# Turning the mixed input by blocks: 32 small DMAs within SBUF, or six by way of a scratch in DRAM

## The chip, the core and the metric

The kernel runs on one core of a Trainium2 chip. The metric is device time in microseconds (us) of one execution. Five engines matter here: PE multiplies matrices, DVE and ACT work elementwise, POOL does a little at the start, and SP issues DMAs, which 16 DMA engines carry out. Each engine works through its own list of instructions in order, and semaphores tie the lists together.

## What is computed

A short dynamic convolution along the sequence, and after it a gated feed-forward layer:

```python
w = np.exp(weight_gen - max); w = w / (sum + 1e-09)      # batch 4, seq 4096, 8 heads, 7 taps
x_unf = x_pad[:, idx, :]                                  # 7 shifted views of x, d_model 192
attn = np.einsum('bshk,bskhg->bshg', w, x_unf)            # 16384 x 192
g = attn @ w_gate                                         # 192 -> 1536
silu = g * (1.0 / (1.0 + np.exp(-g)))
out = (silu * (attn @ w_val)) @ w_out                     # 1536 -> 192
```

## The kernel before

The 16384 tokens are worked through in 32 groups (`NG`) of 512 (`NC`), and each group in 12 steps (`NF`), one for each 128 of the 1536 hidden columns. A step is named here by its f, from 0 to 11. In each step PE makes the 128 gate and 128 value columns for the group's 512 tokens (`up_first` and `up_second`), ACT applies Silu (`sg`, L493), DVE multiplies (`h`, L507), ACT rounds the product to its high part (`hi`, L508), DVE takes the low part (`lo`, L510), and PE, two steps later (`LAG`), multiplies high and low parts by `w_out` (`down`, L537 and L546). Inputs and weights are split into high and low parts as well, so that a product is made of three.

For the next group the convolution runs beside these steps. DVE multiplies and adds seven shifted views of x (`first`, `product`, `add`; L230 and L258), 13 operations that the table `todo` spreads over the steps from f = 9 of one group to f = 5 of the next. The sum has tokens on its partitions, but PE needs the 192 channels there. The turn has these parts:

- `blocks` (L317), at f = 6: DVE transposes 32x32 blocks into the tile `cut`.
- `places` (L330), right behind: SP issues 32 DMAs of 16 KB within SBUF that carry the blocks to their places in the tile `t32` (the profile calls it `t`). Its half 0 holds channels 0 to 127, its half 1 channels 128 to 191 twice, on the upper and the lower 64 partitions.
- `split_ops` (L351, L358): `high(0)` on ACT, `low(0)` on DVE, `high(1)`, `low(1)`. They make `xhi` and `xlo` of both halves. `turn_ops` calls these four the halves.

What sets the order is the code itself: the whole list is written out under a manual schedule. In a step, PE's `up_first` comes first, then the `down` products, `up_second`, Silu and `gated`, which puts the first entry of the step's `todo` list between `hi` and `lo`; the rest of the list follows behind `lo`. With `at` = f 6, the two entries of `moves` stand at `at`, and `halves` are spread from `at + 2` to `at + 4`, that is two at f = 8 and two at f = 9. Group 1 is prepared during group 0 with shorter leads: its turn is at f = 8 and its halves at f = 10 and 11.

Of the next group, `up_first` reads half 1 first: its first two matmuls (L473) need `xhi` of half 1 and the next two `xlo` of half 1. The sums have four PSUM buffers, two for each step, so PE runs up to two steps ahead of `sg` and `h`.

SP's list also holds the loads of x (1344 KB, issued at f = 9 in every second group), of the taps, and the stores of the results (four DMAs a group, at f = 2).

Of the kernel before, what the change touches and what calls it, by code (L numbers as in the profile page):

```python
# [8 lines left out]
F32 = mybir.dt.float32  # L9
# [9 lines left out]
def dynconv_glu_kernel(  # L19
# [23 lines left out]
    nc = tc.nc  # L43
    B, S, D = x.shape
# [3 lines left out]
    P = 128  # L48
    T = B * S // P
    PAD = K - 1  # L50
    DB = D - P
    JG = 4
    NC = JG * P
# [24 lines left out]
    xts = ctx.enter_context(tc.tile_pool(name="xts", bufs=2))  # L78
    hp = ctx.enter_context(tc.tile_pool(name="hp", bufs=2))
    outp = ctx.enter_context(tc.tile_pool(name="outp", bufs=2))  # L80
    ps_up = ctx.enter_context(tc.tile_pool(name="ps_up", bufs=4, space=PSUM))
    ps_dn = ctx.enter_context(tc.tile_pool(name="ps_dn", bufs=1, space=PSUM))

# [35 lines left out]
    def load_taps(c):  # L119

        j0, n = wcuts[c]
        wt = w_t[c] = soft.tile([P, NJ, H, K], F32, tag="wt", name="wt")
        pieces = {0: (0, JG, n), 1: range(0, n + 1, 2 * JG)}.get(c, (0, n))

        def load(a, b):
            nc.sync.dma_start(
                out=wt[:, a:b].rearrange("p t h k -> p t (h k)"), in_=wgr[:, j0 + a : j0 + b]
            )

        return [lambda a=a, b=b: load(a, b) for a, b in zip(pieces, pieces[1:])]  # L130
# [174 lines left out]
    Q = 32  # L305
    NB = D // Q

    def turn_ops(g):

        whole = {}  # L310

        def blocks():
            cut = att.tile([P, JG, D], F32, tag="aside", name="cut", bufs=ASIDE)
            cut = whole["cut"] = cut.rearrange("p t d -> p (t d)").rearrange(
                "p (i t c) -> p i t c", i=NB, t=JG
            )
            nc.vector.transpose(  # L317
                cut, xatt[g][:, :, 0:D].rearrange("p t (i r) -> p i t r", i=NB)
            )

        def places():
            t32 = att.tile([P, JG, 2 * P], F32, tag="xatt", name="t32")
            t32 = whole["t32"] = t32.rearrange("p t d -> p (t d)").rearrange(
                "p (i n) -> p i n", i=2
            )
            for i in range(2 * P // Q):
                half, to = divmod(i * Q, P)
                src = i if i < NB else i - DB // Q
                for j in range(P // Q):
                    nc.sync.dma_start(  # L330
                        out=t32[to : to + Q, half, j * P : (j + 1) * P],
                        in_=whole["cut"][j * Q : (j + 1) * Q, src].rearrange("p t c -> p (t c)"),
                    )

        def part(n):
            def go():
                if n == 0:
                    t32 = whole["t32"]
                    whole["split"] = split_ops(g, (t32[:, 0], t32[:, 1]))
                whole["split"][n]()  # L340

            return go

        return [blocks, places], [part(n) for n in range(4)]

    def split_ops(g, ps):
        hi = [xts.tile([P, NC], F32R, tag=f"xhi{half}", name="xhi") for half in range(2)]

        def high(half):
            def go():  # L350
                nc.scalar.activation(out=hi[half], in_=ps[half], func=AF.Copy)  # L351

            return go

        def low(half):
            def go():
                lo = xts.tile([P, NC], F32R, tag=f"xlo{half}", name="xlo")
                nc.vector.tensor_tensor(  # L358
                    out=lo, in0=ps[half], in1=hi[half].bitcast(F32), op=ALU.subtract
                )  # L360
                xT[g, half] = hi[half], lo

            return go

        return [high(0), low(0), high(1), low(1)]
# [220 lines left out]
    def spread(ops, first, last):  # L586

        for n, op in enumerate(ops):
            at = first + (n * (last - first)) // len(ops)
            todo.setdefault(max(at, 0), []).append(op)  # L590

    with tc.manual_schedule():
        nc.gpsimd.memset(exp_bias, -920.0 * TWO23)

        nc.scalar.activation(out=warm, in_=exp_bias, func=AF.Exp)
        now, soon = load_x(0)
        for op in load_taps(0) + [now]:
            op()
        load_weights(0)
        load_weights(1)  # L600
        soon()
        for f in range(2, RAW):
            load_weights(f)
        make_identity(nc, ident)

        before, exponentials, after = softmax_ops(0)
        for op in before:
            op()
        convert = [weight_ops(f) for f in range(NF)]
        w0, w1, w2, w3 = convert[:4]  # L610
        nc.scalar.activation(out=warm, in_=exp_bias, func=AF.Silu)
        for op in after[:3]:
            op()
        ps, taps = summed_turn(attention_ops(0))
        meanwhile = w0 + w1[:2]
        for op in taps[:2]:
            op()
        for op, other in zip(meanwhile, taps[2:] + [lambda: None]):
            op()
            other()  # L620
        turns = split_ops(0, ps)
        for op in turns[0::2] + w1[2:4] + turns[1:2] + w2[:1] + turns[3:]:
            op()

        later = after[3:]
        loads = load_x(1) + load_taps(1)
        todo[0] = [w2[1], w3[0], w2[2]]
        for i in range(NF):
            ops = todo.setdefault(i, [])
            for f, part in ((i + 2, 3), (i + 3, 1), (i + 4, 0), (i + 3, 2)):  # L630
                if f < NF:
                    ops.append(convert[f][part])
        todo[0] += later[:3]
        spread(loads, LOAD1, LOAD1 + 7)
        spread(later[3:], NF - LEAD - 2, NF - LEAD)
        spread(
            [lambda f=f: split(wo[:, f, 0], wo[:, f, 1], wo32[:, f]) for f in range(NF)],
            WO,
            NF + LAG - 1,
        )  # L640
        for c in range(1, len(wcuts)):
            s0 = (wcuts[c - 1][0] // JG - 1) * NF - LEAD if c > 1 else NF
            s1 = (wcuts[c][0] // JG - 1) * NF - LEAD
            before, exponentials, after = softmax_ops(c)
            at = s0 + (s1 - s0) * 5 // 8 - 2 if c > 1 else EXP1
            if c + 1 < len(wcuts):
                todo.setdefault(s1, []).append(lambda c=c: load_taps(c + 1)[0]())
            spread(before, s0 + 1 - (c == 1), at)
            exps[at] = exponentials
            spread(after, at + 2, s1)  # L650
        for g in range(1, NG):
            s0 = (g - 1) * NF - (LEAD if g > 1 else LEAD1)
            c = first_x.get(g)
            if c and c + 1 < len(xcuts):
                todo.setdefault(s0, []).append(lambda c=c: load_x(c + 1)[0]())
            asides, rest = attention_ops(g)
            spread(asides, max(s0, 0), s0 + NF - 4)
            spread(rest, max(s0, 0), s0 + NF - 3)
            moves, halves = turn_ops(g)
            at = s0 + NF - 3  # L660
            spread(moves, at, at + 1)
            spread(halves, at + 2, at + 4)

        steps = [(g, f) for g in range(NG) for f in range(NF)]
        for i in range(len(steps) + LAG + 1):
            ops = todo.pop(i, [])
            if i < len(steps):
                g, f = steps[i]
                sums, nop = up_first(g, f)
                if i in exps:  # L670
                    exps[i]()
            if i > LAG:
                down(*steps[i - LAG - 1], 1, True)
            late = []
            if LAG <= i < len(steps) + LAG:
                s = steps[i - LAG]
                down(*s, 0, False)
                late = [(*s, 0, True)]
                if s[1]:
                    down(*s, 1, False)  # L680
                else:
                    late.append((*s, 1, False))
            if i < len(steps):
                up_second(g, f, sums, nop)
                sg = silu(sums)
            for what in late:
                down(*what)
            if i > LAG:
                h_t.pop(steps[i - LAG - 1])
            if i < len(steps):  # L690

                def between():
                    if ops:
                        ops.pop(0)()
                    return ops

                gated(g, f, sums, sg, between)
            for op in ops:
                op()
# [33 lines left out]
```

## Time and profile before

| | |
|---|---|
| time, median of 3 runs | 1760.01 us (1759.1 to 1762.0) |
| the profiled execution, its time | 1765.17 us |
| its span, first to last instruction | 1763.4 us |
| PE, DVE, ACT busy | 1420.1, 1026.6, 597.8 us |
| mean granted clock of PE | 0.89 |
| SP's 32 issues of the turn (L330), share of the chain that ended last | 33% |

The profile was taken in one execution; the time around its span is 1.8 us. A clock of 1.00 is 2.4 GHz, 0.50 is 1.2 GHz. The chain that ended last is followed back from the last instruction to whatever released each step, so an engine's share of it is time that set the end. "SPq" is SP's queue at work on issuing.

### The profile page before, as it was taken

To read this page: it belongs to the slowest core of one execution; us is meant where nothing else is said; L and a number is where in the kernel's file an instruction comes from. 1 tells how busy PE (TensorE), PEld (TensorE's weight loads), DVE (VectorE), ACT (ScalarE), POOL (GpSimd) and SP (SyncE) were. 2 spreads that over 40 slices of the span, in tenths; PEclk is the share of its full clock that TensorE was granted. 3 is DMA by queue.
4 is the path that set the end of the run, shared out by engine and by line. 5 is a ranking of instruction groups with operands and counts; after the bars stand their busy time and mean duration, and the time that the engine had idled before them with its cause. 6 is when DMAs were issued, how large, how long until landed. Compare 5 with 4: busy or idle time off the path is not lost.

```text
span 1763.4 us, 32367 instructions
## 1 busy us (share of the span) xinstructions
PE 1420.1 (81%) x13168; PEld 1311.0 (74%) x13168; DVE 1026.6 (58%) x1414; ACT 597.8 (34%) x1048; POOL 61.4 (3%) x62
## 2 busy tenths in 40 slices
PE   5767888878788777888777888777987788988878
PEld 4656788767788766787777787677886777877777
DVE  7946556655556654566555566545566554665543
ACT  4433233433233333333332333332343323333323
POOL 5710000000000000000000000000000000000000
PEclk8988899888899888999888998988998889988899
DMA  5311110111101010111101001111010101100000
GB/s 150 101 50 29 53 22 17 47 22 44 38 20 49 17 53 13 36 35 33 50 19 47 21 17 48 34 44 22 21 46 18 53 13 41 31 16 19 19 16 19
DMA packets 77741, 63.73 MB, mean 36 GB/s; under 512 B 19484, under 2 KB 74780, under 8 KB 75800
## 3 DMA queue, kind: packets, MB, share of 16 engines
q1 hardware_dynamic: 77592, 61.66, 13.2%
q8 instruction: 103, 1.69, 0.4%
q14 instruction: 46, 0.38, 0.1%
HBM read 32.75 MB, written 12.58 MB: 26 GB/s over the span
## 4 chain that ended last, share of the span: by engine, by line
PE 43%; SPq 34%; DVE 12%; ACT 4%; issue 4%; DMA 4%; ACTq 0%; DVEq 0%; POOL 0%
SPq L330 33%; PE up L473 11%; PE up L485 10%; PE dn L537 10%; PE up L476 9%; DMA t<-cut 3%; DVE h L507 3%; PE dn L546 2%; DVE xatt L230 2%; DVE prod L230 2%; DVE cut L317 2%; ACT sg L493 1%; DVE xlo L358 1%; ACT xhi L351 1%; DVE m L423 1%
## 5 line engine op out<-in xcount | busy, mean ns | idle before, releaser
L537 PE MATMUL dn<-wo,hi 64*128 64x384 f32 x2976 | 635.3, 363 | 0.4 <-ACT hi L508 0.4
L546 PE MATMUL dn<-wo,lo 64*128 64x192 f32 x2976 | 555.4, 258 | 0.3 <-DVE lo L510 0.3
L537 PEld LDWEIGHTS dn<-wo,hi 64*128 64x128 f32 x2976 | 531.9, 199 | 14.8 <-ACT hi L508 0.6
L473 PE MATMUL up<-xhi,wb_hi 64*128 64x512 f32 x768 | 276.9, 461 | 313.3 <-ACT sg L493 227.9
L546 PEld LDWEIGHTS dn<-wo,lo 64*128 64x128 f32 x2976 | 493.3, 200 | 5.1 <-DVE lo L510 0.5
L473 PEld LDWEIGHTS up<-xhi,wb_hi 64*128 64x128 f32 x768 | 142.4, 196 | 357.9 <-ACT sg L493 243.0
L507 DVE TENSOR_TENSOR h<-up,sg 128x512 f32<-128x512 f32 x372 | 256.4, 689 | 226.0 <-ACT sg L493 226.0
L508 ACT ACTIVATE hi<-h 128x512 fp32r<-128x512 f32 x372 | 235.1, 632 | 358.9 <-DVE h L507 358.9
L493 ACT ACTIVATE sg<-up 128x512 f32<-128x512 f32 x384 | 227.8, 593 | 340.2 <-PE up L485 306.1
L358 DVE TENSOR_TENSOR xlo<-t,xhi 128x512 fp32r<-128x512 f32 x62 | 42.9, 693 | 428.3 <-ACT xhi L351 415.3
L510 DVE TENSOR_TENSOR lo<-h,hi 128x512 fp32r<-128x512 f32 x372 | 254.8, 685 | 64.2 <-ACT hi L508 64.1
L485 PE MATMUL up<-xhi,wa_hi 64*128 64x512 f32 x768 | 241.8, 440 | 10.4 <-POOLq L275 10.3
L473 PE MATMUL up<-xlo,wb_hi 64*128 64x512 f32 x768 | 248.5, 431 | 1.5 <-DVE xlo L358 1.5
L476 PE MATMUL up<-xhi,wa_lo 64*128 64x512 f32 x768 | 241.4, 422 | 0.0
L473 PE MATMUL up<-xhi,wb_lo 64*128 64x512 f32 x768 | 241.0, 422 | 0.0
L476 PE MATMUL up<-xhi,wa_hi 64*128 64x512 f32 x768 | 240.8, 421 | 0.0
L476 PE MATMUL up<-xlo,wa_hi 64*128 64x512 f32 x768 | 240.5, 420 | 0.0
L485 PE MATMUL up<-xlo,wa_hi 64*128 64x512 f32 x768 | 226.2, 403 | 0.0
L485 PE MATMUL up<-xhi,wa_lo 64*128 64x512 f32 x768 | 224.1, 401 | 0.0
L351 ACT ACTIVATE xhi<-t 128x512 fp32r<-128x512 f32 x62 | 39.0, 629 | 431.0 <-DMA t<-cut 431.0
L230 DVE TENSOR_TENSOR prod<-xt,wt 128x768 f32<-128x768 f32 x183 | 176.3, 963 | 0.2
L258 DVE TENSOR_TENSOR xatt<-xatt,prod 128x768 f32<-128x768 f32 x183 | 176.2, 963 | 0.0
(57 smaller groups left out, 1605.0 us busy)
## 6 DMA issues: line engine op xcount, KB each, us to landing
xt<-in_x_dram SPq DMA_DIRECT2D x14, 1344.0 KB, 5.9
t<-cut SPq DMA_DIRECT2D x992, 16.0 KB, 1.8
out_dram<-osb SPq DMA_DIRECT2D x120, 96.0 KB, 1.9
raw<-in_moe_w_out_dram SPq DMA_DIRECT2D x12, 192.0 KB, 2.7
wt<-in_weight_gen_dram SPq DMA_DIRECT2D x3, 672.0 KB, 4.2
raw<-in_moe_w_gate_dram SPq DMA_DIRECT2D x12, 128.0 KB, 2.1
raw<-in_moe_w_val_dram SPq DMA_DIRECT2D x12, 128.0 KB, 2.3
wt<-in_weight_gen_dram SPq DMA_DIRECT2D x4, 224.0 KB, 3.7
```

The lines of the kernel that those rows point to most:

```text
L230: engine.tensor_tensor(out=into.rearrange("p t (h i) -> p t h i", h=H), in0=src, in1=w, op=ALU.mult)
L258: nc.vector.tensor_tensor(out=a, in0=a, in1=tmp.pop(k), op=ALU.add)
L330: nc.sync.dma_start(out=t32[to : to + Q, half, j * P : (j + 1) * P], in_=whole["cut"][j * Q : (j + 1) * Q, src].rearrange("p t c -> p (t c)"),
L473: nc.tensor.matmul(ps, w[r, fs], m[r], start=(n == 0), stop=False)
L476: ins = nc.tensor.matmul(sums[i], w[r, i, fs], m[r], start=False, stop=False)
L485: ins = nc.tensor.matmul(sums[i], w[r, i, fs], m[r], start=False, stop=(n == len(full) - 1))
L493: nc.scalar.activation(out=sg, in_=sums[0], func=AF.Silu)
L507: nc.vector.tensor_tensor(out=h, in0=sums[1], in1=sg, op=ALU.mult)
L508: nc.scalar.activation(out=hi, in_=h, func=AF.Copy)
L510: nc.vector.tensor_tensor(out=lo, in0=h, in1=hi.bitcast(F32), op=ALU.subtract)
L537: nc.tensor.matmul(acc[t], hi[r, cs], wo[r, f].rearrange("p a d -> p (a d)"), start=opens, stop=False,)
L546: nc.tensor.matmul(acc[t][:, 0:D], lo[r, cs], wo[r, f, 0], start=False, stop=closes)
```

## The change

The 32 DMAs from `cut` to `t32` are replaced. `there` is a scratch in DRAM, 6 x 32 x 4 x 128 numbers, in two buffers. Four DMAs write it, one for each 32 tokens' partitions of `cut`, each with 32 x 6 runs of 512 bytes (96 KB). Two DMAs read it back: 128 rows of 2 KB into half 0, and 64 rows of 2 KB, named twice, into half 1 (256 KB each). For groups 2 and up, the halves move from f = 8 and 9 to f = 9 and 10; for group 1 they stay.

```diff
+    away = ctx.enter_context(tc.tile_pool(name="away", bufs=2, space=bass.MemoryType.DRAM))
...
-            for i in range(2 * P // Q):
-                half, to = divmod(i * Q, P)
-                src = i if i < NB else i - DB // Q
-                for j in range(P // Q):
-                    nc.sync.dma_start(
-                        out=t32[to : to + Q, half, j * P : (j + 1) * P],
-                        in_=whole["cut"][j * Q : (j + 1) * Q, src].rearrange("p t c -> p (t c)"),
-                    )
+            there = away.tile([NB, Q, P // Q, P], F32, tag="turned", name="turned")
+            for j in range(P // Q):
+                nc.sync.dma_start(
+                    out=there[:, :, j].rearrange("i r n -> r i n"),
+                    in_=whole["cut"][j * Q : (j + 1) * Q].rearrange("r i t c -> r i (t c)"),
+                )
+            rows = there.rearrange("i r j n -> (i r) (j n)")
+            nc.sync.dma_start(out=t32[:, 0], in_=rows[0:P])
+            nc.sync.dma_start(
+                out=t32[:, 1], in_=rows[P:D].unsqueeze(0).to_broadcast([2, DB, NC])
+            )
...
-            spread(halves, at + 2, at + 4)
+            spread(halves, at + (2 if g == 1 else 3), at + (4 if g == 1 else 5))
```

SP's list around the turns of two groups, before (`t` is the tile `t32`, its number tells the group's tile apart):

```order
L330 DMA t_2000<-cut 32x128 x32
L140 DMA xt<-in_x_dram 128x2688
L578 DMA out_dram<-osb 32x4x192 x4
L330 DMA t_2644<-cut 32x128 x32
L578 DMA out_dram<-osb 32x4x192 x4
```

and in the changed kernel (`turned` is the scratch):

```order
L329 DMA turned<-cut 32x6x128 x4
L334 DMA t_1952<-turned 128x512
L335 DMA t_1952<-turned 128x1x512
L141 DMA xt<-in_x_dram 128x2688
L582 DMA out_dram<-osb 32x4x192 x4
```

In place of 32 issues stand four writes and two reads; the load of x keeps its place right behind the turn.

DVE's list from the steps f = 8 and 9 of a group, before (`xatt` and `prod` from `xt` and `wt` are the first two operations of the following group's convolution):

```order
L507 TENSOR_TENSOR h<-up,sg 128x512
L510 TENSOR_TENSOR lo<-h,hi 128x512
L358 TENSOR_TENSOR xlo<-t_2644,xhi 128x512
L507 TENSOR_TENSOR h<-up,sg 128x512
L510 TENSOR_TENSOR lo<-h,hi 128x512
L358 TENSOR_TENSOR xlo<-t_2644,xhi 128x512
L230 TENSOR_TENSOR xatt<-xt,wt 128x4x192
L230 TENSOR_TENSOR prod<-xt,wt 128x768
L507 TENSOR_TENSOR h<-up,sg 128x512
```

and in the changed kernel, from f = 9 and 10 of the same group:

```order
L511 TENSOR_TENSOR h<-up,sg 128x512
L514 TENSOR_TENSOR lo<-h,hi 128x512
L362 TENSOR_TENSOR xlo<-t_2571,xhi 128x512
L231 TENSOR_TENSOR xatt<-xt,wt 128x4x192
L231 TENSOR_TENSOR prod<-xt,wt 128x768
L511 TENSOR_TENSOR h<-up,sg 128x512
L514 TENSOR_TENSOR lo<-h,hi 128x512
L362 TENSOR_TENSOR xlo<-t_2571,xhi 128x512
L231 TENSOR_TENSOR prod<-xt,wt 128x768
```

The low part of half 0 now stands ahead of the convolution's first two operations, and that of half 1 behind them. PE's list is the same in both kernels.

## Rows read from the trace of the kernel before

**Rows 1.** The page: busy time, chain by engine, idle time before `xhi`.

```profile
PE 1420.1 (81%) x13168; PEld 1311.0 (74%) x13168; DVE 1026.6 (58%) x1414; ACT 597.8 (34%) x1048; POOL 61.4 (3%) x62
...
PE 43%; SPq 34%; DVE 12%; ACT 4%; issue 4%; DMA 4%; ACTq 0%; DVEq 0%; POOL 0%
...
L351 ACT ACTIVATE xhi<-t 128x512 fp32r<-128x512 f32 x62 | 39.0, 629 | 431.0 <-DMA t<-cut 431.0
```

**Rows 2.** The chain at one group's end: start us, us, what.

```profile
883.99 0.90 DVE cut L317
...
884.90 0.51 SPq L330
...
905.05 1.75 DMA t<-cut
...
906.96 0.64 ACT xhi L351
...
910.70 1.65 PE up L473 x5
```

**Rows 3.** The chain's longest pieces: PE resumes in groups 2 and 31.

```profile
163.38 1.65 PE up L473 x5
...
1711.22 1.64 PE up L473 x5
```

**Rows 4.** Timeline of ACT in the last group: start us, us, instruction, idle before.

```profile
1716.93 0.60 ACT L493 ACTIVATE sg<-up 128x512 f32<-128x512 f32 x1 [3.12 <-PE up L485]
...
1752.25 0.60 ACT L493 ACTIVATE sg<-up 128x512 f32<-128x512 f32 x1 [1.22 <-PE up L485]
```

**Rows 5.** Timeline of PE around one turn, and where group 1 starts.

```profile
885.74 0.41 PE L473 MATMUL up<-xhi,wb_hi 64*128 64x512 f32 x1
...
885.99 0.53 PE L473 MATMUL up<-xlo,wb_hi 64*128 64x512 f32 x2
...
897.99 0.49 PE L473 MATMUL up<-xhi,wb_hi 64*128 64x512 f32 x1 [2.30 <-ACT sg L493]
...
908.12 0.79 PE L473 MATMUL up<-xhi,wb_hi 64*128 64x512 f32 x1 [5.86 <-ACT sg L493]
...
105.73 0.80 PE L473 MATMUL up<-xhi,wb_hi 64*128 64x512 f32 x2 [15.57 <-ACT xhi L351]
```

**Rows 6.** Stretches: width, busy us of five engines, granted clock, DMA share, GB/s.

```profile
898.00:902.00 4.00, 3.65 (x33) 3.07 (x34) 1.47 (x3) 0.63 (x1) 0.00 (x0) 1.00 0.13 28
...
906.00:910.00 4.00, 0.79 (x1) 0.28 (x1) 2.38 (x4) 1.11 (x2) 0.00 (x0) 0.50 0.02 4
```

**Rows 7.** Timeline of ACT, then of DVE, around the same turn.

```profile
882.67 0.60 ACT L493 ACTIVATE sg<-up 128x512 f32<-128x512 f32 x1 [1.23 <-PE up L485]
884.02 0.63 ACT L508 ACTIVATE hi<-h 128x512 fp32r<-128x512 f32 x1 [0.76 <-DVE h L507]
...
889.10 0.60 ACT L493 ACTIVATE sg<-up 128x512 f32<-128x512 f32 x1 [1.23 <-PE up L485]
...
907.62 0.69 DVE L358 TENSOR_TENSOR xlo<-t,xhi 128x512 fp32r<-128x512 f32 x1 [7.45 <-ACT xhi L351]
908.23 0.95 DVE L230 TENSOR_TENSOR xatt<-xt,wt 128x768 f32<-128x768 f32 x1
909.09 0.95 DVE L230 TENSOR_TENSOR prod<-xt,wt 128x768 f32<-128x768 f32 x1
```

**Rows 8.** SP's timeline: four result stores of 96 KB, issued in a row.

```profile
923.44 2.08 SPq L578 DMA_DIRECT2D out_dram<-osb  x4
```

**Rows 9.** DMA issues: count, KB each, us to landing. The stores stand alone (923 to 930).

```profile
out_dram<-osb SPq DMA_DIRECT2D x4, 96.0 KB, 2.6
```

**Rows 10.** The page's DMA issues, two loads of x, medians.

```profile
xt<-in_x_dram SPq DMA_DIRECT2D x14, 1344.0 KB, 5.9
...
xt<-in_x_dram SPq DMA_DIRECT2D x3, 192.0 KB, 2.6
```

**Rows 11.** The DMA queue while only the turn's pieces fly (890 to 904.9 us).

```profile
q1 hardware_dynamic: 1106, 0.38, 11.6%
```

## The prediction

> **What bounds the kernel now.** I read the page first, then the chain of waits, then PE, ACT and DVE around one turn. The page says that PE is busy for 81% of the span, and that SP's queue, which computes nothing, holds 34% of the chain that ended last, while ACT sat idle for 431.0 us ahead of `xhi` until the turn's DMAs landed [rows 1]. The chain of one group shows how: the transpose ends at 884.89, 32 issues follow from 884.90, the last is issued at 905.05 and lands 1.75 later, at 906.80, so half 1 is complete 21.9 us after the transpose; only then come `xhi`, `xlo` and PE [rows 2]. ACT works in order, so `high(0)` and `high(1)`, which wait at f = 8 and 9, hold up the Silus behind them, and PE runs dry: gaps of 2.30 and 5.86 us in this turn [rows 5]. After the second gap the granted clock is 0.50, the 1.2 GHz level; after the first it was still 1.00 [rows 6].
>
> From group 2 to group 31 PE resumes 29 periods apart: (1711.22 - 163.38) / 29 = 53.37 us a group [rows 3]. The last group has no turn to wait for, and there eleven steps take 1752.25 - 1716.93 = 35.32 us, 3.21 each [rows 4]. Twelve such steps are 38.53 us. So 14.8 us of every period are the turn and the slow clock behind it. DVE is no bound in the mean: 1026.6 / 32 = 32.1 us a group [rows 1].
>
> **The change: when the data land.** I count from the end of the transpose.
>
> Writes: four stores of 96 KB are the nearest rows, as large and as finely cut (768 byte runs against 512). Four issue in 2.08 us, 0.52 each [rows 8], so the last write is issued at 1.6; such a store lands 2.6 after its issue [rows 9], at 4.2. SP itself waits there, with the reads and, in every second group, the 1344 KB load of x queued behind. Nobody needs that load before the next group's convolution is through, so this wait costs nothing.
>
> Read 1 is issued at 4.3. The nearest row is the 192 KB load, 2.6 us; the 1344 KB load takes 5.9, which is 72 KB more for each of 16 engines in 3.3 us, 21.8 KB/us [rows 10]. 256 KB are 4 KB more an engine, 0.2 us: read 1 lands at 7.1.
>
> Read 2 is issued 0.65 later (31 spacings in 20.15 us [rows 2]), at 4.9. Spread over all 16 engines, it lands 2.8 later and behind 0.7 of read 1: at 8.4. But it names 64 rows twice, and its outermost count is 2. If only two engines carry it, each has 128 KB instead of 12 (the 192 KB load's share): 116 / 21.8 = 5.3 us more, so 4.9 + 2.6 + 5.3 + 0.7 = 13.5. If pieces of 2 KB went at the rate of the turn's 512 byte pieces, 0.38 MB in 14.9 us x 16 engines x 11.6%, 13.7 KB/us [rows 11], it would be 4.9 + 2.6 + 116 / 13.7 + 16 / 13.7 = 17.2. I take 13.5 as likely and keep 8.4 and 17.2.
>
> **When they are needed.** I take a step's `sg` start as zero. At full rate `hi` follows at 1.35 [rows 7], and PE's `up_first` of the step after next at 3.07, its first `xlo` matmul at 3.32 (885.74 and 885.99 less 882.67) [rows 5, 7]. On DVE a 128x512 operation holds the engine for 0.61 and a convolution operation for 0.87 [rows 7]. The transpose ends at 883.99 + 0.90, 2.2 after `sg` of f = 6 [rows 2, 7]. With the change, `high(0)` has its place at f = 9: three steps and 1.9 later (behind `hi`, 0.63 long), at 11.5. So half 0 has 9.3 us, and needs 7.1: hidden, with 2.2 to spare. At two steps the window would have been 6.1, and the wait would be back.
>
> **What is late next.** DVE. From `sg` of f = 9: `h` 0.63, `lo` 2.01 (after `hi`), `low(0)` 2.62, the first two convolution operations 3.23 and 4.10, free at 4.97. `h` of f = 10 could have begun at 3.84, and begins at 4.97; its `hi` runs 5.69 to 6.32, `high(1)` 6.23 to 6.86, `lo` from 6.35, `low(1)` 6.96 to 7.65. PE would read `xlo` of half 1 at 3.21 + 3.32 = 6.53. It has it at 7.69 and waits 1.16 us, once a group. The clock holds, since a gap of 2.30 left it at 1.00 [rows 5, 6]. `high(1)` can take its data as late as 3 x 3.21 + 6.23 - 2.2 = 13.6 us after the transpose, so 13.5 still hides under this chain, just. In about two groups of six an operation of the softmax stands between as well, 0.87 at most: 0.3 in the mean. The period becomes 38.53 + 1.16 + 0.3 = 40.0.
>
> **The sum.** 29 periods give 29 x (53.37 - 40.0) = 388 us; group 1's own period (163.38 - 105.73) loses the same 13.4. Group 1 starts when its half 1 lands, now 15.57 us of idle PE [rows 5]: 21.9 becomes 13.5, 8 us. The last group's first `sg` came 5.71 after PE resumed at half clock, against 889.10 - 885.74 = 3.36 at full clock [rows 3, 4, 5, 7]: 2.4 more. Together 412 us: the span of 1763.4 becomes 1351, the profiled execution's 1765.2 becomes 1353, and since the median of the runs is 0.3% below that execution, I forecast **1349 us**.
>
> **The rivals.**
>
> *Read 2 lands after `high(1)`'s place.* ACT then waits at f = 10, PE's gap grows by what lies over 13.6, and above some 3 to 5 us the clock falls as it did behind the 5.86 gap. For it: 13.5 stands at the very edge, the source's outermost count is 2, and in every second group the load of x flies beside it. Against it: most rows are those of loads on all engines, by which it is 8.4. At 15.4 the period is 41.8: 1349 + 29 x 1.8 = 1401 us. At 17.2 it is 40.0 + 3.6 + 2.4 = 46.0, about 1525. The Trainium skill, page "DMA: Bandwidth & Descriptors", section "Rules for kernel authors", says that an outermost dimension of c < 16, for instance a zero-stride broadcast of c copies, keeps the whole DMA on at most c engines; with its 27 GiB/s an engine, an estimate from that page would be a landing near 12, still hidden; no row of this trace has such a DMA.
>
> *DVE's chain does not bite.* If PE's wait for `xlo` vanished, because the engines run further ahead than the rows of one step show, the period would be 38.53 and the time 1349 - 29 x 1.5 = 1306 us. Against it: `low(1)` stands behind two convolution operations in DVE's list.
>
> *Slower than before: the broadcast read becomes the new 21.9.* If one engine carried all of its 256 KB at 13.7 KB/us, it would land at 4.9 + 2.6 + 244 / 13.7 + 1.2 = 26.5. PE's gap would be 1.16 + 26.5 - 13.6 = 14.1, with 2.4 of slow clock, a period of 55.3: about 1820 us. It decides from a landing of 24.6 (38.8 + 1.16 + 2.4 + 24.6 - 13.6 = 53.4). Against it: nothing in the rows moves 256 KB so slowly; for it, only that no row has a read of this shape.
>
> **How the numbers follow.** My forecast, 1349 (1325 to 1375): 0.60. Late read, 1375 to 1525: 0.27. No chain: 0.09. Slower: 0.04. The range of 1305 to 1470 takes in the second case up to a landing near 15 and half a step's slow clock, and leaves out the worst of the late read and the slower case, some 0.1. About 0.2% is what a measurement of this kernel can tell from no change. Faster 0.95, same 0.01, slower 0.04.
>
> **What would show it.** Right: SP's queue all but gone from the chain; ACT's wait for the turn's DMAs below 30 us in total; a new wait of PE for `xlo` (L362) of about 1.2 us in 30 groups; a granted clock above 0.97; periods near 40. Read 2's time to landing tells its engines: near 3.5 us means sixteen, 8 to 9 two. Wrong: ACT idle ahead of the second `xhi` of each group, a clock still near 0.9, or periods of 45 and more, would mean that half 1 lands after its place; a wait ahead of the first `xhi`, that writes or read 1 cost more than the rows say.

## The result, and the profile after

The changed kernel takes **1362.65 us** (median of 4 runs, 1358.95 to 1363.24), the kernel before 1760.05 us beside it: a ratio of 0.7737, interval [0.7721, 0.7752]. The forecast was 1349, with 1325 to 1375 as its own range. The profiled execution has a span of 1361.4 us at a mean granted clock of 0.985, against 1763.4 at 0.890.

First the page of the changed kernel: busy time, the granted clock in 40 slices, the chain by engine, and two kinds of DMA with their size and their median time to landing.

```profile
PE 1289.9 (95%) x13168; PEld 1129.5 (83%) x13168; DVE 1025.6 (75%) x1414; ACT 599.8 (44%) x1048; POOL 61.9 (5%) x62
...
PEclk9889899999999999999999999999999999999999
...
PE 67%; DVE 14%; DMA 8%; ACT 6%; issue 3%; SPq 2%; ACTq 0%; DVEq 0%
...
xt<-in_x_dram SPq DMA_DIRECT2D x14, 1344.0 KB, 11.6
t<-turned SPq DMA_DIRECT2D x62, 256.0 KB, 2.6
```

SP's queue held 34% of the chain [rows 1] and holds 2%; PE has gone from 43% to 67% of it. Read the last two lines with care: the load of x, an instruction that the change did not touch, now lands 11.6 us after its issue instead of 5.9 [rows 10]. And the 2.6 us of `t<-turned` are those of read 1 alone, since the landings of read 2 are not in that median; read 2 has to be read from the chain.

The waits of the changed kernel: who, at which line, for whom; total us, times, longest us.

```profile
ACT xhi L355 <- DMA t<-turned: 9.4, 7, 4.2
...
PE up L477 <- ACT xhi L355: 20.1, 31, 6.0
...
PE up L477 <- DVE xlo L362: 16.9, 30, 3.2
...
DVE mx L170 <- DMA wt<-in_weight_gen_dram: 10.8, 6, 3.7
```

ACT waits 9.4 us for the turn, where it sat idle for 431.0 before [rows 1]. PE has two new waits of about the same size, first for `xhi` (20.1 us, 31 times, 6.0 of it where group 1 starts) and then for `xlo` (16.9 us, in 30 groups); the prediction named the second alone. The last line, DVE's `mx` behind a load of taps, is the one that the prediction did not have.

Now the timeline of the changed kernel around an ordinary group end (start us, us, instruction, idle before). `sg` at 946.25 is that of f = 9.

```profile
946.25 0.60 ACT L497 ACTIVATE sg<-up 128x512 f32<-128x512 f32 x1 [1.22 <-PE up L489]
...
948.15 0.62 ACT L355 ACTIVATE xhi<-t 128x512 fp32r<-128x512 f32 x1
...
951.22 0.68 DVE L511 TENSOR_TENSOR h<-up,sg 128x512 f32<-128x512 f32 x1
...
952.48 0.61 ACT L355 ACTIVATE xhi<-t 128x512 fp32r<-128x512 f32 x1
...
953.15 0.51 PE L477 MATMUL up<-xhi,wb_hi 64*128 64x512 f32 x2 [0.31 <-ACT xhi L355]
953.22 0.68 DVE L362 TENSOR_TENSOR xlo<-t,xhi 128x512 fp32r<-128x512 f32 x1
...
953.96 0.50 PE L477 MATMUL up<-xlo,wb_hi 64*128 64x512 f32 x2 [0.30 <-DVE xlo L362]
...
993.63 0.50 PE L477 MATMUL up<-xlo,wb_hi 64*128 64x512 f32 x2 [0.32 <-DVE xlo L362]
```

Counted from `sg`, `h` of f = 10 begins at 4.97, `high(1)` at 6.23 and `low(1)` at 6.97: the prediction has 4.97, 6.23 and 6.96. No idle time stands before either `xhi`, so neither half's data are late here. The two idle notes of PE, 0.31 for `xhi` and 0.30 for `xlo`, look like 0.61 us, but the ends of matmuls are modelled. The weight loads of the same two rows are noted with 0.54 and 0.62 idle, 1.16 together, and the period tells the true loss: 993.63 - 953.96 = 39.67, against 38.53 for twelve steps, so 1.14 us. Fourteen of the 28 periods from group 2 to group 30 are between 39.67 and 39.70; the other half are longer, up to 42.28. The mean of all 28 is (1273.17 - 144.64) / 28 = 40.30, from the first and the last of these `xlo` rows.

One of the long ones, around 387 us, in the chain, the timeline and the stretch behind the gap (its columns are width, busy us of five engines, granted clock, DMA share, GB/s):

```profile
374.79 0.49 SPq L335
...
375.32 9.92 DMA wt<-in_weight_gen_dram
```

```profile
385.26 0.86 DVE L170 TENSOR_REDUCE mx<-wt 128x96 f32<-128x672 f32 x1 [1.29 <-DMA wt<-in_weight_gen_dram]
...
386.63 0.69 DVE L362 TENSOR_TENSOR xlo<-t,xhi 128x512 fp32r<-128x512 f32 x1
...
387.37 0.50 PE L477 MATMUL up<-xlo,wb_hi 64*128 64x512 f32 x2 [1.65 <-DVE xlo L362]
```

```profile
388.00:392.00 4.00, 4.00 (x30) 3.52 (x29) 3.12 (x5) 0.63 (x1) 0.00 (x0) 0.60 0.00 0
```

SP issues read 2 (L335) and right behind it the load of taps, which lands 9.9 us later. In DVE's list `mx`, which reads the taps, stands ahead of `lo` and `low(1)`, so `xlo` is late, PE idles 1.65 us (and 0.31 for `xhi` just before), and the granted clock of the next stretch is 0.60. This group's period is 41.04 and the next one's 41.25.

And the chain where the load of x flies beside the turn: the transpose ends at 898.41, read 2 is issued from 903.80 and lands 9.06 later.

```profile
897.51 0.90 DVE cut L318
...
899.75 3.52 DMA turned<-cut
...
903.41 0.34 SPq L334
...
903.80 9.06 DMA t<-turned
912.88 0.64 ACT xhi L355
```

That is 14.45 us after the transpose, past the 13.6 that `high(1)` could give it. Two things are late here. Read 2 takes longer beside the load of x, and the last write lands 4.86 us after the transpose, so that read 1 is issued at 5.00. This second delay is not the rule: in 24 of the 31 groups read 1 is issued 3.4 to 3.7 us after the transpose. Why the writes are late in the other seven was not looked into.

What the experiments had to settle: whether the gain comes from the six DMAs, from the moved steps, or only from both; whether read 2's two engines are the cause of the long periods; and whether the ordinary 1.14 us are DVE's chain.

### The profile page after: what moved, and what is told of

The parts are those of the page before. It is cut to its first block, busy times and chain, and to the rows that moved or that the text cites. A ratio compares the mean times of both kernels' runs of the same rounds, so it can differ in the third digit from the quotient of the medians.

```text
span 1361.4 us, 31191 instructions
## 1 busy us (share of the span) xinstructions
PE 1289.9 (95%) x13168; PEld 1129.5 (83%) x13168; DVE 1025.6 (75%) x1414; ACT 599.8 (44%) x1048; POOL 61.9 (5%) x62
## 4 chain that ended last, share of the span: by engine, by line
PE 67%; DVE 14%; DMA 8%; ACT 6%; issue 3%; SPq 2%; ACTq 0%; DVEq 0%
PE up L477 15%; PE up L489 15%; PE dn L541 15%; PE up L480 14%; PE dn L550 7%; DMA t<-turned 3%; DVE h L511 3%; DMA wt<-in_weight_gen_dram 3%; DVE xlo L362 3%; ACT hi L512 2%; ACT sg L497 2%; DVE prod L231 2%; DVE xatt L231 1%; DMA turned<-cut 1%; SPq L329 1%
## 5 line engine op out<-in xcount | busy, mean ns | idle before, releaser
L541 PE MATMUL dn<-wo,hi 64*128 64x384 f32 x2976 | 479.8, 346 | 0.4 <-ACT hi L512 0.4
L550 PE MATMUL dn<-wo,lo 64*128 64x192 f32 x2976 | 393.9, 249 | 0.3 <-DVE lo L514 0.3
L541 PEld LDWEIGHTS dn<-wo,hi 64*128 64x128 f32 x2976 | 302.6, 185 | 29.2 <-ACT hi L512 0.6
L550 PEld LDWEIGHTS dn<-wo,lo 64*128 64x128 f32 x2976 | 302.6, 187 | 28.4 <-DVE lo L514 0.5
L477 PE MATMUL up<-xhi,wb_hi 64*128 64x512 f32 x768 | 176.0, 425 | 24.9 <-ACT xhi L355 20.1
L477 PE MATMUL up<-xlo,wb_hi 64*128 64x512 f32 x768 | 165.5, 402 | 16.9 <-DVE xlo L362 16.9
L489 PE MATMUL up<-xhi,wa_hi 64*128 64x512 f32 x768 | 169.7, 419 | 11.3 <-POOLq L276 11.2
L480 PE MATMUL up<-xhi,wa_lo 64*128 64x512 f32 x768 | 161.5, 394 | 0.0
L480 PE MATMUL up<-xhi,wa_hi 64*128 64x512 f32 x768 | 161.1, 392 | 0.0
L480 PE MATMUL up<-xlo,wa_hi 64*128 64x512 f32 x768 | 160.6, 391 | 0.0
L489 PE MATMUL up<-xhi,wa_lo 64*128 64x512 f32 x768 | 159.3, 392 | 0.0
L489 PE MATMUL up<-xlo,wa_hi 64*128 64x512 f32 x768 | 158.4, 390 | 0.0
L480 PEld LDWEIGHTS up<-xlo,wa_hi 64*128 64x128 f32 x768 | 80.6, 186 | 16.8
## 6 DMA issues: line engine op xcount, KB each, us to landing
xt<-in_x_dram SPq DMA_DIRECT2D x14, 1344.0 KB, 11.6
```

The source lines that it names most:

```text
L477: nc.tensor.matmul(ps, w[r, fs], m[r], start=(n == 0), stop=False)
L480: ins = nc.tensor.matmul(sums[i], w[r, i, fs], m[r], start=False, stop=False)
L489: ins = nc.tensor.matmul(sums[i], w[r, i, fs], m[r], start=False, stop=(n == len(full) - 1))
L541: nc.tensor.matmul(acc[t], hi[r, cs], wo[r, f].rearrange("p a d -> p (a d)"), start=opens, stop=False,)
L550: nc.tensor.matmul(acc[t][:, 0:D], lo[r, cs], wo[r, f, 0], start=False, stop=closes)
```

## Experiments

**The six DMAs with the old steps.** The changed kernel, with the halves back at f = 8 and 9.

```diff
-            spread(halves, at + (2 if g == 1 else 3), at + (4 if g == 1 else 5))
+            spread(halves, at + 2, at + 4)
```

> The six DMAs by way of DRAM, but with the halves back at f = 8 and 9. Theory: the three steps are as needed as the shorter turn. In the changed kernel half 0 lands 7.6 us and half 1 13 to 14.5 us after the transpose; at f = 8 and 9 their places come after 6.1 and 9.3 us, so ACT waits some 1.5 us ahead of the first xhi and 4 us ahead of the second, PE's gap grows by 3 to 4.5 us a group and the clock falls after it: periods near 44.5, about 1480 us (1450 to 1510). Rival, the shorter turn alone is what pays and ACT's lead over PE swallows the rest: about 1363, as the changed kernel.

Measured: 1419.42 us (1411.37 to 1423.24), ratio to the kernel before 0.8055 [0.8027, 0.8083]; the profiled execution is the one of 1411.37, at clock 0.974. Its waits, two of its PE rows and the stretches behind them, and the chain of an ordinary group:

```profile
ACT xhi L355 <- DMA t<-turned: 116.7, 48, 4.2
...
PE up L477 <- DVE h L511: 56.9, 34, 2.1
```

```profile
817.12 0.64 PE L477 MATMUL up<-xhi,wb_hi 64*128 64x512 f32 x1 [2.09 <-DVE h L511]
...
900.73 0.49 PE L477 MATMUL up<-xhi,wb_hi 64*128 64x512 f32 x1 [1.78 <-DVE h L511]
```

```profile
817.00:821.00 4.00, 3.88 (x24) 3.41 (x26) 3.97 (x8) 1.75 (x3) 0.00 (x0) 0.57 0.00 0
901.00:905.00 4.00, 4.00 (x44) 3.57 (x44) 4.00 (x7) 1.95 (x4) 0.00 (x0) 1.00 0.02 4
```

```profile
1264.28 0.90 DVE cut L318
...
1266.54 2.03 DMA turned<-cut
...
1269.00 7.99 DMA t<-turned
```

The wait that the prediction foresaw for two steps of lead is there: ACT waits for the turn 48 times, 116.7 us. But I had priced it too high, by 60 us. The gaps that reach PE are about 2 us, shorter than the 3 to 4.5 that I had assumed, and the clock falls behind some of them (0.57 from 817 us) and not behind others (1.00 from 901), where I had let it fall behind all; the mean of 0.974 says that the latter are the rule. One reason for the shorter gaps is that half 1 lands earlier than I had taken it to. The DMAs are those of the changed kernel, and here ACT waits for half 1 in every group, so that its landing can be read. In the group shown the transpose ends at 1265.18, the last write lands 3.4 us later, read 2 is issued at 3.8 and lands at 11.8. In the eleven groups in which no load is issued behind read 2 and the writes are on time it is 11.3 to 12.2, beside a load of x or of taps 12.2 to 13.2, and 12.2 to 14.4 in the six in which the reads are issued late. So most of the change's gain is the six DMAs (1760 to 1419); the later steps bring 57 us more.

**The later steps with the old 32 DMAs.** The kernel before, with the halves at f = 9 and 10.

```diff
-            spread(halves, at + 2, at + 4)
+            spread(halves, at + (2 if g == 1 else 3), at + (4 if g == 1 else 5))
```

> The 32 DMAs within SBUF as before, but the halves at f = 9 and 10 for groups 2 and up. Theory: a turn that takes 21.9 us does not fit in 13.6. ACT waits about 2 us ahead of the first xhi and 6 to 8 ahead of the second, PE has a gap of 9 us with slow clock behind it: periods near 50, about 1665 us (1630 to 1690). Rival, the later steps are the whole gain, since they let PE run through the issues: below 1450 us.

Measured: 1701.08 us (1698.78 to 1701.38), ratio 0.9657 [0.9641, 0.9673], clock 0.886. Its waits:

```profile
PE up L473 <- ACT xhi L351: 297.0, 32, 14.1
...
ACT xhi L351 <- DMA t<-cut: 284.3, 62, 8.3
...
DVE mx L169 <- DMA wt<-in_weight_gen_dram: 40.2, 6, 9.5
```

PE's periods shrink from 53.37 us to 51.2, 2.2 of the 3.21 that one step of lead is worth; a landing 21.9 us after the transpose is still late, and the wait stays. The run is 11 us over the top of what I expected, and DVE's waits for the taps are a likely reason: the taps' load stands behind the 32 issues in SP's list, and with the halves one step later `low(1)` is behind `mx` in DVE's. Of their 40.2 us, 27.4 are three waits, one in each of three groups, and the three periods that hold them are 54.3 to 54.4 us, where the other 26 have 50.8 in the mean: 10.7 us together. It is the same term that was missing from the prediction. The taps were not moved apart from the rest, so this stays a reading of the trace.

**Read 2 as two plain reads.** The changed kernel, with 64 rows read twice instead of one read that names them twice.

```diff
-            nc.sync.dma_start(
-                out=t32[:, 1], in_=rows[P:D].unsqueeze(0).to_broadcast([2, DB, NC])
-            )
+            for to in (0, DB):
+                nc.sync.dma_start(out=t32[to : to + DB, 1], in_=rows[P:D])
```

> The changed kernel with read 2, which names its 64 rows twice, written as two reads of 64 rows each (128 KB each, seven DMAs a group). Theory: read 2 runs on two engines only, lands 7.6 to 9.1 us after its issue, and holds up the loads of x and of the taps that are queued behind it. With two plain reads each lands in about 3 us, the 1344 KB load takes about 6 us again instead of 11.6, ACT's waits for the turn (9.4 us) and DVE's waits for the taps (10.8 us) go, and with them the long gaps in groups 1, 2, 8 and 14 and the clock they cost: about 1344 us (1338 to 1352). PE's wait of 1.16 us a group stays, so the shortest periods remain 39.7. Rival, the read is slow because DRAM has just been written: the landing stays at 7 us or more and the time at 1363.

Measured: 1339.09 us (1338.98 to 1339.41), ratio 0.7605 [0.7594, 0.7616], clock 0.993; 23.6 us less than the changed kernel. Its DMAs and one of its waits:

```profile
xt<-in_x_dram SPq DMA_DIRECT2D x14, 1344.0 KB, 6.7
...
t<-turned SPq DMA_DIRECT2D x62, 128.0 KB, 3.2
```

```profile
DVE mx L170 <- DMA wt<-in_weight_gen_dram: 3.7, 2, 2.9
```

Each half of the same 256 KB now lands 3.2 us after its issue, and with them the load of x falls from 11.6 to 6.7 and `mx`'s wait from 10.8 to 3.7: both were held up behind read 2. PE's rows, one where group 1 starts and two of ordinary groups, show what is left:

```profile
92.06 0.50 PE L476 MATMUL up<-xhi,wb_hi 64*128 64x512 f32 x2 [1.70 <-ACT xhi L354]
...
612.55 0.50 PE L476 MATMUL up<-xlo,wb_hi 64*128 64x512 f32 x2 [0.30 <-DVE xlo L361]
...
652.22 0.50 PE L476 MATMUL up<-xlo,wb_hi 64*128 64x512 f32 x2 [0.32 <-DVE xlo L361]
```

The ordinary period is 39.67, as in the changed kernel, so read 2 has no part in the 1.14 us. From 134.50 to 1249.07 the mean of 28 periods is 39.81: 0.50 less than 40.30, which is 14.0 us. Group 1 starts at 92.06 instead of 96.98, 4.9 us, and the period from group 1 to 2 is 5.2 shorter. Together 24.1 of the 24.2 us between the two spans. Of the 28 periods four are longer, by 0.8 to 1.0 (40.48 to 40.69); they are those in which ACT makes the softmax's exponentials, for which it first loads a table:

```profile
268.19 1.28 ACT L183 ACT_TABLE_LOAD   x1
269.49 1.33 ACT L183 ACTIVATE wt<-wt 128x1344 f32<-128x1344 f32 x1
```

**The convolution one step later.** The changed kernel, with the convolution's operations from f = 10 on, behind `low(1)`; read 2 is as it was.

```diff
-            spread(rest, max(s0, 0), s0 + NF - 3)
+            spread(rest, max(s0, 0) if g == 1 else s0 + 1, s0 + NF - 3)
```

> The changed kernel with the convolution of the next group spread from f = 10 instead of f = 9 (groups 2 and up), so that its first two operations no longer stand ahead of the low part of half 1. Read 2 stays as it is. Theory: DVE's chain costs PE 1.16 us a group, but read 2 lands hardly earlier (13.1 us after the transpose in ordinary groups, 14.5 beside a load), so that about half of it is given back: about 1352 us (1346 to 1358), with a new wait of ACT for the second half's DMA in most groups. Rival, the chain alone sets PE's wait: about 1330 us (1325 to 1338).

Measured: 1350.59 us (1349.47 to 1351.27), ratio 0.7669 [0.7658, 0.7681]. Its waits, and its chain in a group that has no load of x beside it but late writes:

```profile
ACT xhi L355 <- DMA t<-turned: 23.3, 22, 4.7
...
PE up L477 <- DVE xlo L362: 13.4, 18, 3.2
```

```profile
694.07 0.90 DVE cut L318
...
700.26 8.03 DMA t<-turned
```

The wait for `xlo` goes in 12 groups, and ACT's wait for read 2 takes its place: 22 times instead of 7. In the group shown half 1 lands 708.29 - 694.97 = 13.3 us after the transpose, because read 2 is issued at 5.3. Where the writes are on time and no load flies beside, half 1 lands at about 11.8, as in the run with the old steps, and is not late. So the edit pays in part of the groups: 12 of the 28 periods are 38.6 to 39.0, that is 0.7 to 1.1 below 39.67, and the others are longer, up to 42.3. In the changed kernel, then, two things are late at nearly the same moment wherever a load or late writes hold up read 2, and taking away DVE's chain shows the other. The 28 periods win 0.50 each, 13.9 us, where the chain alone would be worth 28 x 1.14 = 31.9; the run as a whole wins 12.

**Both edits together.** Two plain reads, and the convolution one step later.

```diff
-            nc.sync.dma_start(
-                out=t32[:, 1], in_=rows[P:D].unsqueeze(0).to_broadcast([2, DB, NC])
-            )
+            for to in (0, DB):
+                nc.sync.dma_start(out=t32[to : to + DB, 1], in_=rows[P:D])
...
-            spread(rest, max(s0, 0), s0 + NF - 3)
+            spread(rest, max(s0, 0) if g == 1 else s0 + 1, s0 + NF - 3)
```

> Both at once: read 2 as two plain reads, and the next group's convolution from f = 10. Theory: the chain on DVE and the late half 1 covered for each other, so that only both edits together remove PE's wait of 1.16 us. The low part of half 1 would be ready at 6.56 us after the Silu of f = 9, PE wants it at 6.53: periods of 38.6, 1339 - 28 x 1.1 = about 1308 us (1303 to 1316). Rival, another wait takes its place, since DVE now has 13 convolution operations to fit in eight steps: 1330 or more.

Measured: 1315.21 us (1313.92 to 1317.24), ratio 0.7458 [0.7443, 0.7473]. Its chain by engine, and the first `xhi` of two neighbouring groups on ACT's timeline:

```profile
PE 87%; DVE 7%; ACT 2%; issue 1%; DMA 1%; SPq 0%; DVEq 0%; ACTq 0%
```

```profile
874.06 0.62 ACT L354 ACTIVATE xhi<-t 128x512 fp32r<-128x512 f32 x1
...
912.60 0.62 ACT L354 ACTIVATE xhi<-t 128x512 fp32r<-128x512 f32 x1
```

The period is 912.60 - 874.06 = 38.54, twelve steps of 3.21: with half 1 early and the convolution out of the way, nothing of the turn is left on PE's path. That settles that the 1.14 us are DVE's chain. With read 2 early the later convolution is worth 23.9 us (1339.09 - 1315.21), against 12 with it late. Over the 28 periods it is 1.00 each, 28.1 us, against the 13.9; some 6 us are lost again at the start, most of them in group 1's period, which grows from 41.6 to 46.3.

**Both edits' gain with the convolution in its place.** Two plain reads land early enough for all four halves to stand at f = 9, ahead of the convolution's first operations.

```diff
-            nc.sync.dma_start(
-                out=t32[:, 1], in_=rows[P:D].unsqueeze(0).to_broadcast([2, DB, NC])
-            )
+            for to in (0, DB):
+                nc.sync.dma_start(out=t32[to : to + DB, 1], in_=rows[P:D])
...
-            spread(halves, at + (2 if g == 1 else 3), at + (4 if g == 1 else 5))
+            spread(halves, at + (2 if g == 1 else 3), at + 4)
```

> Two plain reads, the convolution again from f = 9, but all four halves at f = 9 (groups 2 and up). Theory: with both halves landing about 9 us after the transpose, the second xhi has its place at 9.9 us and need not wait; low(1) stands ahead of the convolution's first two operations, so PE's wait for xlo goes: periods of 38.6 to 38.8, about 1309 us (1303 to 1318). The product h of f = 10 then begins at 5.6 us after the Silu of f = 9 and ends at 6.3, just as PE needs its buffer. Rival, the second half is late for f = 9 and the wait is back: periods of 40 and more, 1345.

Measured: **1307.22 us** (1306.94 to 1307.68), ratio 0.7416 [0.7405, 0.7427], clock 0.990. It is the fastest version, 55 us below the changed kernel. Its busy time and its chain by engine, and the two `xhi` of neighbouring groups:

```profile
PE 1267.7 (97%) x13168; PEld 1240.5 (95%) x13168; DVE 1020.4 (78%) x1414; ACT 597.8 (46%) x1048; POOL 61.2 (5%) x62
...
PE 89%; DVE 5%; ACT 3%; DMA 1%; issue 1%; SPq 0%; DVEq 0%; ACTq 0%
```

```profile
555.47 1.14 ACT L354 ACTIVATE xhi<-t 128x512 fp32r<-128x512 f32 x2
...
594.00 1.14 ACT L354 ACTIVATE xhi<-t 128x512 fp32r<-128x512 f32 x2
```

Again 38.53 a group; PE's own rate sets the time. The gain over the run with plain reads alone is 1339.09 - 1307.22 = 31.9 us, just the 28 x 1.14 of DVE's chain. So three steps of lead are enough for both halves. With read 2 on two engines half 1 lands 11.8 us after the transpose in an ordinary group, behind the 9.9 of this place; the fourth step, for `high(1)`, was there for that read. All halves at f = 9 with that read was not run.

## Why the prediction was right, step by step

- **The bound.** That 14.8 us of every period were the turn and the slow clock behind it was the base of the sum. The fastest version, whose turn is off PE's path, runs at 38.53 us a group, the full rate that was read from the last group [rows 4].
- **The writes and read 1.** In an ordinary group the last write lands at 3.4 (forecast 4.2), read 1 is issued at 3.5 (4.3) and lands 2.6 later, at 6.1 (7.1). The write was sized too long: it takes 2.03 from the start of its issue, where I took 2.6 from one row of result stores [rows 9]; the page of the kernel before has 1.9 as the median of all 120 such stores. In the slow groups it is too short: in the group at 898 the last write lands at 4.86 and read 1 at 7.6. All of it is under the window of 9.3, so from group 2 on half 0 is hidden, as forecast.
- **Read 2.** I took 13.5, for two engines, between 8.4 and 17.2; an ordinary group has 11.8, a group with the load of x beside it 12.4 to 13.2, one with late writes up to 15.0. Two engines was right, and the size was 1.7 too large: 1.1 from the reads' earlier issue (3.8 instead of 4.9), 0.6 from the read itself (8.0 instead of 8.6). The forecast did not suffer, since anything below 13.6 hides behind DVE's chain; that the term could be off without being seen is luck. In the changed kernel's stretch from 947 to 948 us, in which read 2 flies alone, the row is:

```profile
947.00:948.00 1.00, 1.00 (x14) 0.87 (x12) 0.58 (x1) 0.39 (x1) 0.00 (x0) 1.00 0.13 47
```

  A DMA share of 0.13 is 2 of 16 engines, and 47 GB/s are 23.5 for each, near the 21.8 that I had from the two loads of x. The 8.0 to 9.1 us from issue are in the band that I had named for two engines, and as plain reads each half of the data takes 3.2. The Trainium skill, page "DMA: Bandwidth & Descriptors", section "Rules for kernel authors", says that a leading broadcast of c copies keeps a DMA on at most c engines: by that share the trace agrees. The estimate from that page's 27 GiB/s, a landing near 12, was nearer than mine, in part because the reads were issued earlier than both assumed; the engines' 23.5 GB/s are less than that figure.
- **DVE's chain.** Its three begins came within 0.01 us. PE's loss was forecast as 1.16 and is 1.14. About half of it is PE's wait for `xhi` of half 1, which is late by the same chain (its `hi` waits for `h`) and which the prediction did not name. The rival without this chain (1306) is out: with read 2 early and nothing else moved the ordinary period stays at 39.67, and it falls to 38.5 both times that `low(1)` stands ahead of the convolution's first operations.
- **The clock.** It was to hold behind a gap of 1.2 us, and does: 1.00 in the stretches of the ordinary group, 0.985 in the mean. The reason given, that a gap of 2.30 had left it at 1.00, does not hold in general: it fell to 0.60 behind the 1.65 at 388 us. The rival's 3 to 5 us as the gap that brings the clock down is not borne out either.
- **The start and the end.** Group 1's start was to come 8 us earlier, and comes at 96.98 instead of 105.73 [rows 5], 8.75. From the last group's start to the end of the span it is 49.6 us instead of 52.2, 2.6 against the forecast 2.4. Group 1's own period was to lose 13.4 and loses 10.0, from 56.9 to 46.9.
- **The rivals.** A late read 2 came about in part: 7 waits, 9.4 us in total. Three are in groups 1 and 2 (6.1 us), the other four in groups in which the writes are late and the load of x flies beside read 2. In the periods the longest of these waits is 1.37, a landing of 13.6 + 1.37 = 15.0, and the rival was worked out for 15.4 and more in every group. The slower case, a landing of 24.6, is far off.

What was mis-sized is the difference of 13.7 us. Over the span it is 10.4 (1361.4 against 1351), and of these the 28 periods have 8.5 (40.30 instead of 40.0) and group 1's period 3.4, while the last period, the start and the end give back 2.3; the rest is the rounding of the sum. The other 3.3 come from the last step of the sum, which set the median 0.3% below the profiled execution; after the change the two agree (1361.4 and 1.8 around it, against 1362.65). Within the period two terms are off, in opposite directions:

- **What stands behind read 2 in SP's list was costed at nothing.** The step says of SP's wait that "Nobody needs that load before the next group's convolution is through, so this wait costs nothing". That holds for x: nobody waits for it at 11.6 us either. It was not asked of the loads of taps, which DVE's `mx` reads ahead of `low(1)`; nor does the sum hold the other direction, that the load of x holds up read 2 (9.06 from its issue in the group at 898, against 7.99 in the ordinary group). With plain reads both are gone, and with them 0.50 us a period, 14.0 us in 28.
- **The softmax term was wrong in kind.** I had put 0.3 us into every period for softmax operations in DVE's list. In the run with plain reads the ordinary groups have 39.67 with or without them: they fit into the time in which DVE waits for `hi`. What the softmax does cost falls in the periods with ACT's exponentials, 0.8 to 1.0 us in four of them, 3.8 us in place of 28 x 0.3 = 8.4. That it is the exponentials and their table load is read from where they stand and was not tried apart.

So 40.0 should have read 38.53 + 1.14 + 0.14 + 0.50 = 40.3.

## What to carry to other kernels

When issuing bounds a move of data, a detour by DRAM in few large DMAs can beat many small ones on the chip, and it is priced by when each part lands against the place of its reader, not by its bytes. Read the list of the DMA queue past the instruction that changes: here what stood behind a DMA that two engines carried was late as well, and its reader stood ahead of the work that mattered. Where two things are late at the same moment, an experiment that takes away one can show less than its worth (here 13.9 us of 28.1 in the periods); take away both before you judge either. And look at more than one group before you call a landing ordinary.

## What was not expected of the hardware

A DMA on two engines delays DMAs that are issued behind it on the same queue: the 1344 KB load lands after 11.6 us instead of 5.9 to 6.7, though the two engines' share is 0.13 of all.

The granted clock is not ordered by the length of PE's gap alone. Behind a gap of 1.65 us, with one of 0.31 just before, it was 0.60 (388 us, changed kernel) and behind one of 2.09 it was 0.57 (817 us, old steps), yet behind 1.78 us it was 1.00 (901 us, old steps), and so it was behind 2.30 us in the kernel before [rows 5, 6]. What decides was not tried apart and stays open.
